# One more batch without PE transposes, and duplicated keys beside kept zeros in a thresholded attention and RWKV feed-forward

## The chip, the cores and the metric

The kernel runs on one core of a Trainium2 chip. A core has five engines that run their own instruction streams side by side: PE (TensorE, matmuls and their weight loads, PEld), DVE (VectorE), ACT (ScalarE), POOL (GpSimd) and SP (SyncE, which here only issues DMA transfers). They meet through semaphores. The metric is the device time of one execution in microseconds; the kernel before takes 974.39 us, the median of three runs (973.27 to 975.24).

## The reference

Two stages follow each other. Eight batches of eight heads, 576 positions, head width 64; then a feed-forward layer of width 512 to 1024 and back over the same 8 x 576 rows.

```python
scores = scale * np.matmul(q, k.transpose(0, 1, 3, 2))
thresh = np.max(scores, axis=-1, keepdims=True) - tau
scores = np.where(scores >= thresh, scores, -1000000000.0)
attn = np.exp(scores - np.max(scores, axis=-1, keepdims=True))
attn = attn / (np.sum(attn, axis=-1, keepdims=True) + 1e-09)
x = np.matmul(attn, v)                      # heads side by side: 512 columns
x_prev = x shifted by one row, zeros first
xk = mu_k * x + (1.0 - mu_k) * x_prev       # xr likewise with mu_r
k = np.maximum(xk @ w_k, 0.0)
out = sigmoid(xr @ w_r) * ((k * k) @ w_v)
```

A score that misses the threshold by a little is dropped altogether, so the scores have to be nearly as exact as float32.

## The kernel before, in words

**Jobs and units.** A job is one batch and one pair of heads (`hp`, four pairs in a batch). Its queries are worked in units: a P unit is 128 query rows for each of the two heads (two softmaxes of 128 x 576), the T unit is the 64 last rows of both heads together (one softmax). A whole job has one T and four P units, so nine softmaxes; a batch has 36 and the program 288. The first `HALF` batches are halved: each of their jobs is cut into two jobs with two P units in the first and T with two P units in the second, which lets the feed-forward of the first 256 rows start early. Before, `HALF` is 2, so there are 16 half jobs and 24 whole ones, 40 in all.

**Scores.** In the first `PLAIN` jobs the scores are plain float32 matmuls straight from the loaded tile `raw` (L600). In the others ACT rounds the tile to the PE's fast type (`hl`, the high part, L510), POOL takes the rest (the low part, L520), and DMA copies stack both parts so that one matmul with 128 rows of contraction does two products. Before, `st1` holds high and low of queries and keys in alternating partitions and `st2` holds the queries with the two parts exchanged; the products are `st1` by `st1` and `st2` by `st1` (L617). T units take another form (L590).

**Softmax of a unit**, per head: row maximum on DVE (L657), threshold on ACT (L665), exponential on ACT (L673), mask, product and sum in one DVE instruction (L681), reciprocal on DVE (L701), scaling on POOL (L710).

**Turning the probabilities.** The matmul with V wants them transposed. Batches below `MOVED` do it on PE: four 128 x 128 transposes for each head of a P unit (L739) into a PSUM tile `w`, which ACT or DVE then copies out into `pm` (L755, L757). Batches from `MOVED` on are "turned" without PE: DVE transposes 32 x 32 blocks of both heads in one instruction (L775; L839 for T), one DMA writes the block rows to DRAM (`far`, `near`; L810, L849), and another reads them back in the order of a full transpose (L815, L860). The tile `pt` that DVE turns into has one buffer (`TB`). A last piece of 64 columns is turned on PE in every unit. Before, `MOVED` is 2, so 24 jobs are turned.

**Attention output and feed-forward.** `attend` multiplies by V (L906). Its result is copied to `xT` by DVE (L757). When the four pairs of a half batch are done, `ffn_chunk` works 256 rows: POOL and ACT mix the rows (L999 to L1045), PE multiplies by `w_k` (L1067, 96 matmuls), `w_r` (L1109, 24) and `w_v` (L1131, 48), with ACT, POOL and DVE between them. A batch has two such chunks, and every four batches one more for the last rows.

**Weights.** 20 pieces of the three weight matrices are fetched and split into high and low parts on POOL, ACT and DVE (L421 to L465) while the first two batches run.

**What sets the order.** Every instruction is first entered as a `Step` with an engine, an expected duration and a key. `Plan.order` then walks through time: on each engine, of the steps whose inputs are there, the one that can start first goes next, and of equals the one with the smaller key. What comes out is a fixed instruction stream for each engine; nothing is reordered on the chip. PE prefers scores, turns and attention (key less 1000) to feed-forward matmuls, so the feed-forward of a batch fills PE while the attention of the next one goes on. Steps at L1191 ("turnstile") transpose the identity for nothing, in the first 100 us of the plan, where PE would otherwise stand idle.

## Time and profile before

| | |
|---|---|
| median of three runs | 974.39 us (973.27 to 975.24) |
| the profiled execution, its own time | 972.76 us |
| span of the trace (first to last instruction) | 970.9 us |
| busy, share of the span | PE 96%, PEld 79%, DVE 71%, ACT 75%, POOL 70% |
| mean granted PE clock | 0.994 of full speed |
| DMA | 227.41 MB, mean 234 GB/s |

The 1.86 us between the span and the execution's own time lie outside the instructions. The chain of work that ended last runs 62% of the span over PE, 17% over DMA, 8% over ACT, 6% over DVE and 3% over POOL. Busy times of a group of instructions are unions of intervals: matmuls overlap, so the time that one more matmul costs is read from the distance of starts, not from the mean length of one.

### The profile page before, as it was taken

To read this page: it belongs to the slowest core of one execution; us is meant where nothing else is said; L and a number is where in the kernel's file an instruction comes from. 1 tells how busy PE (TensorE), PEld (TensorE's weight loads), DVE (VectorE), ACT (ScalarE), POOL (GpSimd) and SP (SyncE) were. 2 spreads that over 40 slices of the span, in tenths; PEclk is the share of its full clock that TensorE was granted. 3 is DMA by queue.
4 is the path that set the end of the run, shared out by engine and by line. 5 is a ranking of instruction groups with operands and counts; after the bars stand their busy time and mean duration, and the time that the engine had idled before them with its cause. 6 is when DMAs were issued, how large, how long until landed. Compare 5 with 4: busy or idle time off the path is not lost.

```text
span 970.9 us, 17935 instructions
## 1 busy us (share of the span) xinstructions
PE 936.5 (96%) x6142; PEld 768.9 (79%) x6142; DVE 689.1 (71%) x1424; ACT 728.7 (75%) x1569; POOL 678.9 (70%) x834
## 2 busy tenths in 40 slices
PE   9888899999999999999999999999999999999998
PEld 8666687887868787878887878788878878878886
DVE  6978897777778687878798868787877777830120
ACT  5899989898777878677868696868777778764432
POOL 3899978676776776958767677676767677664541
PEclk9999999999999999999999999999999999999999
DMA  5696455436768788788878778888778787750000
GB/s 190 235 323 251 150 178 176 161 133 235 267 238 325 275 313 302 279 295 283 299 257 294 240 281 306 278 299 298 276 295 282 262 275 266 266 197 23 22 22 22
DMA packets 91514, 227.41 MB, mean 234 GB/s; under 512 B 8480, under 2 KB 24352, under 8 KB 85280
## 3 DMA queue, kind: packets, MB, share of 16 engines
q1 hardware_dynamic: 91424, 226.27, 66.2%
q8 instruction: 49, 0.80, 0.4%
q14 instruction: 41, 0.34, 0.1%
HBM read 102.77 MB, written 66.06 MB: 174 GB/s over the span
## 4 chain that ended last, share of the span: by engine, by line
PE 62%; DMA 17%; ACT 8%; DVE 6%; POOL 3%; issue 2%; SPq 1%; ACTq 0%; POOLq 0%; DVEq 0%
PE w L1131 14%; PE w L1067 14%; PE w L906 12%; PE s L617 9%; PE w L1109 7%; DMA pm<-far 7%; DMA far<-pt 6%; PE w L739 4%; DVE pt L775 2%; DMA st<-hl 2%; ACT p L673 2%; DMA near<-pt 2%; PE s L590 2%; DVE p L681 1%; PE w L1191 1%
## 5 line engine op out<-in xcount | busy, mean ns | idle before, releaser
L681 DVE SCALAR_TENSOR_TENSOR p<-s,sm,p 128x576 f32<-128x576 f32 x288 | 232.2, 811 | 70.1 <-ACT p L673 68.9
L657 DVE TENSOR_REDUCE sm<-s 128x1 f32<-128x576 f32 x288 | 212.4, 749 | 53.3 <-PE s L617 36.0
L710 POOL TENSOR_SCALAR p<-p,sm 128x576 f32<-128x576 f32 x288 | 212.5, 749 | 38.4 <-DVE sm L701 32.4
L1067 PE MATMUL w<-xk,wk 128*128 128x256 f32 x1728 | 227.9, 283 | 1.7 <-ACT pl L755 1.1
L1067 PEld LDWEIGHTS w<-xk,wk 128*128 128x128 f32 x1728 | 216.4, 188 | 3.7 <-ACT pl L755 1.4
L1131 PE MATMUL w<-wv,k 128*128 128x512 f32 x864 | 219.0, 398 | 0.0
L673 ACT ACTIVATE p<-s,sm 128x576 f32<-128x576 f32 x288 | 210.3, 733 | 8.3 <-DVE pt L775 7.4
L1131 PEld LDWEIGHTS w<-wv,k 128*128 128x128 f32 x864 | 156.8, 189 | 33.3 <-issue 1.8
L906 PE MATMUL w<-pm,v 128*64 128x256 f32 (+1 forms) x1024 | 140.0, 415 | 8.2 <-DMA pm<-far 5.1
L1090 POOL TENSOR_TENSOR k<-r,k 128x512 fp32r<-128x512 f32 x72 | 92.7, 1288 | 51.6 <-ACT k L1080 50.4
L775 DVE STREAM_TRANSPOSE pt<-p 128x1024 f32<-128x1024 f32 x96 | 115.5, 1228 | 17.9 <-DMA near<-pt 8.5
L665 ACT ACTIVATE sm<-sm,small 128x1 f32<-128x1 f32 x288 | 83.3, 290 | 51.5 <-DVE sm L657 50.5
L617 PE MATMUL s<-st 128*128 128x288 f32 x496 | 114.9, 313 | 6.3 <-DVE p L681 5.2
L906 PEld LDWEIGHTS w<-pm,v 128*64 128x64 f32 x1024 | 70.7, 138 | 60.8 <-issue 6.7
L693 POOL TENSOR_SCALAR sm<-sm 128x2 f32<-128x2 f32 (+1 forms) x160 | 30.7, 192 | 115.9 <-DVE p L681 101.8
L1109 PE MATMUL w<-wr,xk 128*128 128x512 f32 x432 | 110.5, 396 | 0.0
L520 POOL TENSOR_TENSOR hl<-raw,hl 128x576 fp32r<-128x576 f32 (+2 forms) x76 | 103.6, 1385 | 9.8 <-ACT hl L510 9.4
L617 PE MATMUL s<-st,st 128*128 128x288 f32 x496 | 109.2, 302 | 0.7 <-DMA st<-hl 0.6
L617 PEld LDWEIGHTS s<-st 128*128 128x128 f32 x496 | 81.3, 190 | 31.8 <-DVE p L681 11.2
L739 PE MATMUL w<-ident,p 128*128 128x128 f32 x448 | 83.9, 284 | 10.2 <-ACT pm L755 3.2
L1109 PEld LDWEIGHTS w<-wr,xk 128*128 128x128 f32 x432 | 76.9, 188 | 14.1 <-issue 0.8
L617 PEld LDWEIGHTS s<-st,st 128*128 128x128 f32 x496 | 79.5, 189 | 2.8 <-issue 1.5
(74 smaller groups left out, 1204.2 us busy)
## 6 DMA issues: line engine op xcount, KB each, us to landing
far<-pt SPq DMA_DIRECT2D x48, 1024.0 KB, 5.6
pm<-far SPq DMA_DIRECT2D x48, 1024.0 KB, 5.7
st<-hl SPq DMA_DIRECT2D x48, 576.0 KB, 4.3
raw<-in_qk SPq DMA_DIRECT2D x24, 608.0 KB, 6.4
v<-in_v SPq DMA_DIRECT2D x40, 320.0 KB, 3.9
st<-hl SPq DMA_DIRECT2D x28, 448.0 KB, 3.2
st<-hl SPq DMA_DIRECT2D x96, 128.0 KB, 3.1
out<-sg SPq DMA_DIRECT2D x32, 256.0 KB, 3.0
```

Of the source, the lines that this page charges most:

```text
L520: lambda cs=cs: G.tensor_tensor(hl.get()[:, 1, cs], raw.get()[:, cs], hl.get()[:, 0, cs].bitcast(F32), op=ALU.subtract),
L617: PE.matmul(ss[y].get()[:, z, 0:HS], l.get()[:, c * P : (c + 1) * P], r.get()[:, keys(y, z)], start=(j == 0), stop=(j == 1),)
L657: lambda sv=sv, col=col: V.tensor_reduce(col(0), sv(), axis=AX.XY, op=ALU.max, negate=True),
L673: lambda sv=sv, pv=pv, col=col: A.activation(pv(), sv(), AF.Exp, bias=col(0)),
L681: lambda sv=sv, pv=pv, col=col: V.scalar_tensor_tensor(pv(), sv(), col(1), pv(), op0=ALU.is_ge, op1=ALU.mult, accum_out=col(2)),
L710: lambda y=y, o=y * S if unit["kind"] == "P" else 0: G.tensor_scalar(p.get()[:, o : o + S], p.get()[:, o : o + S], sm.get()[:, 3, y : y + ...
L739: PE.transpose(pt.get()[:, c, :], x(), ident.get())
L775: V.transpose(o, x)
L906: PE.matmul(o.get()[hs, 0:n], vt.get()[:, c, hs], pt, start=(c == 0), stop=(c == 4))
L1067: PE.matmul(h.get()[:, f], l, r, start=(ct == 0 and i == 0), stop=(ct == NCT - 1 and i == 2))
L1109: PE.matmul(z.get(), l, r, start=(ct == 0 and i == 0), stop=(ct == NCT - 1 and i == 2))
L1131: PE.matmul(vps.get(), l, r, start=(ft == 0 and i == 0), stop=(ft == NFT - 1 and i == 2))
```

## The change

Three parts. First, constants: `HALF` 2 to 1 (batch 1 is no longer halved: 8 half jobs and 28 whole ones), `PLAIN` 2 to 4 (the whole first half of batch 0 has plain scores; its jobs 2 and 3 borrow the buffers of `xk`), `MOVED` 2 to 1 (batch 1 is turned too). Second, the stacked tiles: `st1` now holds high and low of the queries and, behind them, the high part of the keys twice; `st2` holds the low part of the keys in every other partition and zeros between, which are written once by two memsets and kept. The products are `st1` by the doubled keys and `st1` by `st2`, so three of the four products of before are computed and low by low falls away. Third, keys and expected durations of the plan, which give a new order on every engine.

```diff
-MOVED = 2
-PLAIN = 2
+MOVED = 1
+PLAIN = 4
...
-    HALF = 2
-    W0, W1, W2, W3, AVK = 5, 3, 50, 2, 1.5
-    PREP, PB, VB, COLD, EARLY = 12, 3, 1, -1, 30
+    HALF = 1
+    W0, W1, W2, W3, AVK = 3, 4, 60, 1.5, 4.5
+    PREP, PB, VB, COLD, EARLY = 8, 3, 1, -1, 30
...
-        job["st"] = [(sbuf("st1", [P, WM - ST], FR, 3), sbuf("st2", [P, SM], FR, 2)) for _ in range(2)]
+        job["st"] = [(sbuf("st1", [P, SM + S], FR, 3), sbuf("st2", [P, S], FR, 2)) for _ in range(2)]
...
-                    t1.get()[:, 0 : W - qt].bitcast(F32), hl.get()[h::2, :, qt:W].bitcast(F32)
+                    t1.get()[:, 0 : nq - qt].bitcast(F32), hl.get()[h::2, :, qt:nq].bitcast(F32)
...
+            def high(t1=t1, h=h, k0=k0):
+                x = hl.get()[h::2, 0, k0 : k0 + S].bitcast(F32)
+                x = bass.AP(x.tensor, x.offset, [list(x.ap[0]), [0, 2], list(x.ap[1])])
+                SY.dma_start(t1.get()[:, nq - qt : nq - qt + S].bitcast(F32), x)
...
+                    t2.get()[0::2, :].bitcast(F32), hl.get()[h::2, 1, k0 : k0 + S].bitcast(F32)
...
+                        r = st2.get() if j else st1.get()[:, nq - qt : nq - qt + S]
                         PE.matmul(
                             ss[y].get()[:, z, 0:HS],
                             l.get()[:, c * P : (c + 1) * P],
-                            r.get()[:, keys(y, z)],
+                            r[:, z * HS : (z + 1) * HS],
...
                 evict(
-                    *EV[y if n > EARLY else 0],
+                    *EV[y],
...
-    wat = [6 + 1 * j for j in range(len(wlist))]
+    wat = [2 + 3 * j for j in range(len(wlist))]
```

`EV` gives the engine that copies PE transposes out: ACT for head 0, DVE for head 1. Before, ACT took both heads in the first units (`n` up to `EARLY`). `wat` holds the keys of the weight pieces.

**Place 1: PE in the second half of batch 1's scores.** `s` are score tiles, `p` probability tiles, `w` PSUM tiles; L739 before is L761 now (a transpose), L617 is L639, L1131 is L1153, L590 is L611. Before, between softmax 48 and 51:

```order
L739 MATMUL w_97<-ident,p_1654 128x128 x4
L739 MATMUL w_93<-ident,p_1654 128x128 x4
L739 MATMUL w_89<-ident,p_1654 128x128
L617 MATMUL s_128<-st_0_1713 128x288 x2
L617 MATMUL s_128<-st_0_1713,st_0_1695 128x288 x2
L617 MATMUL s_130<-st_1_1735 128x288 x2
L617 MATMUL s_130<-st_1_1735,st_1_1723 128x288 x2
L1109 MATMUL w_97<-wr_0_962,xk_667 128x512 x3
L739 MATMUL w_103<-ident,p_1721 128x128 x4
L739 MATMUL w_89<-ident,p_1721 128x128 x4
L739 MATMUL w_93<-ident,p_1721 128x128
```

Now, between softmax 52 and 54, in the same batch:

```order
L761 MATMUL w_93<-ident,p_1568 128x128
L1153 MATMUL w_101<-wv_0_1687,k_0_1212 128x512 x3
L1153 MATMUL w_101<-wv_0_1692,k_0_1212 128x512 x3
L761 MATMUL w_97<-ident,p_1619 128x128
L761 MATMUL w_93<-ident,p_1668 128x128
L1153 MATMUL w_107<-wv_0_1687,k_0_1212 128x512 x3
L1153 MATMUL w_101<-wv_0_1705,k_0_1212 128x512 x3
L639 MATMUL s_134<-st_1_1289 128x288 x2
L639 MATMUL s_134<-st_0_83,st_1_1289 128x288 x2
L639 MATMUL s_136<-st_2_1484 128x288 x2
L639 MATMUL s_136<-st_1_85,st_2_1484 128x288 x2
```

The groups of four transposes are gone, the single ones for the last 64 columns stay, and `w_v` matmuls of batch 0's feed-forward stand where they were. Counted up to the scores of softmax 73 (the first of batch 2): L739 has 319 transposes before and 182 now; L1067 186 and 192 matmuls, L1109 24 and 48, L1131 48 and 78.

**Place 2: DVE in batch 1.** L657 now L679 is the maximum, L681 now L703 the mask, L757 now L779 a copy out of PSUM, L775 now L797 the turn; L436, L444 and L454 (now L441, L449, L459) belong to a weight piece. Before:

```order
L657 TENSOR_REDUCE sm_1569<-s_130 128x1
L444 SCALAR_TENSOR_TENSOR w_89<-xT_80,w_89 128x512
L681 SCALAR_TENSOR_TENSOR p_1588,sm_1569<-s_128,sm_1569,p_1588 128x576
L454 SCALAR_TENSOR_TENSOR xT_80<-xT_80,w_89 128x512
L757 COPY xT_80<-w_97 128x256
L681 SCALAR_TENSOR_TENSOR p_1588,sm_1569<-s_130,sm_1569,p_1588 128x576
L757 COPY pm_406<-w_89 128x4x4x32
L701 RECIPROCAL sm_1569<-sm_1569 128x2
```

Now:

```order
L679 TENSOR_REDUCE sm_1478<-s_136 128x1
L459 SCALAR_TENSOR_TENSOR xT_80<-xT_80,w_97 128x512
L797 STREAM_TRANSPOSE pt_1422<-p_1368 128x2x4x128
L703 SCALAR_TENSOR_TENSOR p_1429,sm_1398<-s_134,sm_1398,p_1429 128x576
L703 SCALAR_TENSOR_TENSOR p_1499,sm_1478<-s_136,sm_1478,p_1499 128x576
L441 TENSOR_SCALAR w_107<-wv_0_975 128x512
L723 RECIPROCAL sm_1398<-sm_1398 128x2
L679 TENSOR_REDUCE sm_1478<-s_134 128x1
L679 TENSOR_REDUCE sm_1554<-s_136 128x1
```

A turn stands between the masks in place of a copy to `pm`. Up to the mask of softmax 36 DVE has 8 copies out of PSUM and 14 finished weight pieces before, 22 copies (16 of them to `pm`) and 13 pieces now; from there to the mask of softmax 72 it has 31 copies and 6 pieces before, and 15 copies, 7 pieces, 14 turns at L775 and 4 at L839 now.

**Place 3: SP, the stacked tiles and the trips to DRAM.** Before, in the first turned job (batch 2):

```order
L546 DMA st_0_2697<-hl_2632 128x1x1152
L481 DMA raw_2701<-in_qk 128x1216
L849 DMA near_2708<-pt_2703 128x512
L498 DMA v_2715<-in_v 128x640
L860 DMA pm_208<-near_2708 128x4x128
L535 DMA st_0_2774<-hl_2632 64x512 x2
L546 DMA st_1_2784<-hl_2632 128x1x1152
L810 DMA far_2806<-pt_2758 128x2048
```

Now, in batch 1, where its first job is turned and its second and third get their tiles:

```order
L567 DMA st_0_83<-hl_1279 64x576
L549 DMA st_2_1484<-hl_1279 128x1x512
L561 DMA st_2_1484<-hl_1279 128x1x576
L832 DMA far_1518<-pt_1422 128x2048
L567 DMA st_1_85<-hl_1279 64x576
L837 DMA pm_215<-far_1518 128x4x512
L561 DMA st_0_1610<-hl_1598 128x1x576
L549 DMA st_0_1610<-hl_1598 128x1x512
L832 DMA far_1649<-pt_1596 128x2048
L496 DMA raw_1656<-in_qk 128x1216
```

One transfer of 1152 columns and two of half the partitions became one of 512, one of 576 and one of half the partitions for each head. Over the whole program DVE has 16 more turns of L775 and 4 more of L839, SP 16 more of each of L810 and L815 and 4 more of each of L849 and L860; L739 has 144 transposes fewer (448 to 304), copies of them out of PSUM fall from 54 to 20 on ACT and from 18 to 16 on DVE, and the turnstile has 156 transposes in place of 174.

## Rows read from the trace of the kernel before

**Rows 1.** The page's first part: busy time, share of the span and instructions of each engine.

```profile
PE 936.5 (96%) x6142; PEld 768.9 (79%) x6142; DVE 689.1 (71%) x1424; ACT 728.7 (75%) x1569; POOL 678.9 (70%) x834
```

**Rows 2.** Busy time by stretches of the span. Columns: stretch, its length, then for PE, PEld, DVE, ACT and POOL the busy us and the instructions, the granted PE clock, the DMA engines' share and GB/s.

```profile
0.00:54.00 54.00, 47.74 (x340) 37.90 (x340) 40.26 (x87) 39.95 (x89) 35.04 (x51) 1.00 0.63 221
54.00:108.50 54.50, 46.29 (x309) 34.70 (x307) 45.60 (x101) 51.36 (x120) 51.62 (x67) 0.97 0.70 256
108.50:210.70 102.20, 98.81 (x716) 82.13 (x715) 80.99 (x178) 89.45 (x202) 78.67 (x99) 0.98 0.50 169
210.70:316.60 105.90, 102.06 (x653) 82.34 (x652) 81.49 (x164) 83.29 (x181) 75.92 (x94) 0.98 0.71 252
316.60:857.10 540.50, 532.41 (x3495) 438.39 (x3494) 424.06 (x856) 416.33 (x901) 388.43 (x479) 1.00 0.80 281
857.10:970.90 113.80, 109.21 (x641) 93.47 (x639) 16.72 (x46) 48.34 (x81) 49.22 (x48) 1.00 0.15 49
```

**Rows 3.** The same stretches, the masks at L681 alone (each counts twice, with the read of its sum behind it): DVE busy, clock, DMA.

```profile
0.00:54.00 54.00, 13.02 (x32) 1.00 0.63 221
54.00:108.50 54.50, 16.33 (x42) 0.97 0.70 256
108.50:210.70 102.20, 29.40 (x74) 0.98 0.50 169
```

**Rows 4.** The same stretches, the turnstile (L1191) alone: PE and PEld busy, clock, DMA.

```profile
0.00:54.00 54.00, 21.05 (x147) 19.03 (x147) 1.00 0.63 221
54.00:108.50 54.50, 3.56 (x29) 3.10 (x27) 0.97 0.70 256
```

**Rows 5.** PE in order of time around 660 us. Columns: start, length, engine, line, operation, tiles, shape, count.

```profile
658.67 2.38 PE L1067 MATMUL w<-xk,wk 128*128 128x256 f32 x18
660.88 0.43 PE L617 MATMUL s<-st 128*128 128x288 f32 x2
```

**Rows 6.** The same view around 215 us.

```profile
214.56 0.60 PE L739 MATMUL w<-ident,p 128*128 128x128 f32 x4
214.91 0.52 PE L617 MATMUL s<-st 128*128 128x288 f32 x2
215.27 0.43 PE L617 MATMUL s<-st,st 128*128 128x288 f32 x2
215.53 0.43 PE L617 MATMUL s<-st 128*128 128x288 f32 x2
...
216.78 2.31 PE L1109 MATMUL w<-wr,xk 128*128 128x512 f32 x9
219.03 2.37 PE L906 MATMUL w<-pm,v 128*64 128x320 f32 x16
```

**Rows 7.** The same view at a plain job's scores.

```profile
7.71 1.24 PE L600 MATMUL s<-raw 64*128 64x288 f32 x8
8.88 3.82 PE L1191 MATMUL w<-ident 128*128 128x128 f32 x33
```

**Rows 8.** Groups of instructions by line and shape: busy us, mean ns of one, then the idle time before them and what ended it.

```profile
L739 PE MATMUL w<-ident,p 128*128 128x128 f32 x448 | 83.9, 284 | 10.2 <-ACT pm L755 3.2 <-POOL p L710 3.0 <-DVE xT L454 1.6
...
L775 DVE STREAM_TRANSPOSE pt<-p 128x1024 f32<-128x1024 f32 x96 | 115.5, 1228 | 17.9 <-DMA near<-pt 8.5 <-DMA far<-pt 5.3 <-POOL p L710 3.8
...
L755 ACT ACTIVATE pm<-w 128x512 f32<-128x512 f32 x54 | 31.7, 597 | 9.9 <-PE w L739 9.2
...
L839 DVE STREAM_TRANSPOSE pt<-p 128x512 f32<-128x512 f32 x24 | 17.0, 707 | 8.3 <-DMA far<-pt 6.6 <-POOL sm L693 1.0 <-POOL p L710 0.7
...
L454 DVE SCALAR_TENSOR_TENSOR xT<-xT,w 128x512 uint32<-128x512 uint32 x20 | 13.6, 679 | 0.1
...
L757 DVE COPY pm<-w 128x512 f32<-128x512 f32 x18 | 12.4, 687 | 3.2 <-PE w L739 3.0
```

**Rows 9.** Busy time by stretches again, columns as in rows 2, for three stretches of 25 us in the first 150.

```profile
25.00:50.00 25.00, 21.41 (x156) 14.92 (x156) 22.19 (x47) 21.97 (x51) 21.29 (x30) 1.00 0.68 239
...
75.00:100.00 25.00, 19.64 (x118) 15.02 (x117) 22.13 (x49) 23.59 (x55) 23.29 (x31) 0.93 0.59 210
...
125.00:150.00 25.00, 24.63 (x193) 21.58 (x192) 23.41 (x51) 22.41 (x51) 20.00 (x25) 1.00 0.49 166
```

**Rows 10.** Who waited for whom: total us, times, longest us. SPq is the DMA queue of SP.

```profile
DVE pt L775 <- DMA near<-pt: 8.5, 11, 1.4
...
DVE pt L839 <- DMA far<-pt: 6.6, 9, 1.4
...
DVE pt L775 <- DMA far<-pt: 5.3, 8, 1.2
...
PE w L906 <- DMA pm<-far: 5.1, 9, 1.0
...
PE s L617 <- DMA st<-hl: 1.4, 4, 0.6
...
SPq L815 <- DMA far<-pt: 119.6, 39, 6.2
```

**Rows 11.** DMA issues: tiles, queue, count, size of one, median us from issue to landing.

```profile
far<-pt SPq DMA_DIRECT2D x48, 1024.0 KB, 5.6
pm<-far SPq DMA_DIRECT2D x48, 1024.0 KB, 5.7
st<-hl SPq DMA_DIRECT2D x48, 576.0 KB, 4.3
```

More of the change, by code (lines that the diff above doesn't have):

```diff
@@ L81 @@
     HOP, LATE, FROM = 0.09, 0.3, 200.0
-    SOFT = {"DVE": 0.3, "ACT": 0.15, "POOL": 0.2}
-    IDLE = 0.5
+    SOFT = {"DVE": 0.15, "ACT": 0.15, "POOL": 0.2}
+    IDLE = 0.7
     def __init__(self):
@@ L105, in add @@
         s.ready = wait
+        if key > -500 and until is None:
+            s.key += AMP * ((s.idx * 2654435761 + SEED * 40503) % 65536 / 65536 - 0.5)
         def split(x):
@@ L470, in weight @@
         plan.soft = False
+    for j in range(2):
+        t2 = sbuf("st2", [P, S], FR, 2)
+        add("DVE", 0.3, lambda t2=t2: V.memset(t2.get().bitcast(F32), 0.0), writes=[t2], key=-97)
     def operands(job, key):
@@ L476, in operands @@
         W = nq + 2 * ST + SM
-        raw = job["raw"] = sbuf("raw", [P, WM], F32) if job["ji"] != 1 else sbuf("k2", [P, 2 * NFT * CH], F32)
+        raw = job["raw"] = (
+            sbuf("k2", [P, 2 * NFT * CH], F32)
+            if job["ji"] == 1
+            else sbuf("xk", [P, 2 * NCT * CH], F32, 2)
+            if job["ji"] in (2, 3)
+            else sbuf("raw", [P, WM], F32)
+        )
         add(
@@ L612, in scores, with mm @@
             st1, st2 = job["st"][y]
-            for j, l in enumerate((st1, st2)):
-                def mm(j=j, l=l, r=st1, y=y):
+            for j in range(2):
+                def mm(j=j, l=st1, y=y, st1=st1, st2=st2):
                     for z in range(2):
+                        r = st2.get() if j else st1.get()[:, nq - qt : nq - qt + S]
                         PE.matmul(
```

50 lines of the change are left out of this document (25 added, 25 removed).

## The prediction

> **What bounds the kernel now.** I read the page's busy shares first. PE stands at 96% of the span, the next engine at 75% [rows 1]; that alone says little, since lengths of matmuls overlap. So second the busy time by stretches, cut at the batches: the masks count 37 up to 108.5 us and 37 more up to 210.7 us [rows 3], so these are batch 0 and batch 1. From 316.6 to 857.1 us PE is busy 532.4 of 540.5 us [rows 2]. Third the starts on PE: 18 matmuls of the kind L1067 take from 658.67 to 660.88 us, 0.123 us each without a gap [rows 5]. From the third batch on PE is full, and a microsecond of PE work more or less there is a microsecond of time.
>
> The first two batches differ. Up to 108.5 us PE is busy 94.0 us, of which 24.6 us are turnstile, transposes for nothing [rows 2, 4]; it does useful work for about 69 us. There the other engines set the pace: between 75 and 100 us ACT is busy 23.59 of 25 us, POOL 23.29, DVE 22.13 [rows 9]. Over batch 0 ACT has 91.3 us, POOL 86.7, DVE 85.9 [rows 2]: ACT is the fullest, with 17.2 us idle. In batch 1 PE is at 98.81 of 102.2 us, ACT at 89.45, DVE at 80.99.
>
> The Trainium skill (Perfetto Trace Analysis, Identifying the Most-Contended Engine) says that matmul busy time doesn't tell how near PE is to its limit, and takes the busy time of weight loads instead. By that measure PE is at 438.4 of 540.5 us, 81%, from 316.6 us on [rows 2], and removed transposes would fall into free time. The gapless starts of rows 5 speak against it, so it is a rival below, not my reading.
>
> **PE work.** In batch 1, 36 groups of four transposes go (144 of 448). In rows 6 such a group starts at 214.56 and the next instruction at 214.91, 0.35 us; the pair of score matmuls behind it takes 0.36 us to its successor where the next pair takes 0.26. So a group costs 0.35 + 0.10 = 0.45 us, and 36 cost 16.2 us. The bounds are 0.35 (12.6 us) and the busy time over the count, 83.9 us / 448 x 4 = 0.75 (27 us) [rows 8], which counts overlap; I take 0.45. The four units that become plain take 8.88 - 7.71 = 1.17 us [rows 7] where four pairs took 4 x 0.265 = 1.06 [rows 6], together 0.4 us more. The new stacked products have as many matmuls of the same size: nothing. PE gets 15.8 us less to do. Were the time in which it stands or turns idly unchanged, the span would be 970.9 - 15.8 = 955.1 us.
>
> **Whether PE loses more time in the first two batches.** That depends on DVE, which gets the turns. Row durations overlap a little: the page's 689 us of DVE are 0.92 of their sum, so I scale by that.
>
> Batch 0: 16 copies to pm come over from ACT to DVE (0.687 us each, +11.0), two copies to xT (about 0.4) and one weight piece (three instructions like L454, 0.68 each) come later: +8.1, scaled +7.4 us [rows 8]. DVE has 93.3 us, ACT loses those copies (16 x 0.597 = 9.6) and falls to about 82 or below. DVE takes ACT's place with 2 us more work. With ACT's 17.2 us of idleness the batch ends at 110.5 us in place of 108.5.
>
> Batch 1: DVE gets 14 x 1.228 + 4 x 0.707 = 20.0 us of turns before the mask of softmax 72, 2.1 for a weight piece, and loses 16 copies, 11.0: +11.1, scaled +10.2 [rows 8]. That is 81.0 + 10.2 = 91.2 us. DVE has run at 89% and 94% of a stretch when work was at hand (22.19 and 23.41 of 25 us [rows 9]); at 92% the batch takes 99.1 us and ends at 209.6 us, 1.1 before the old 210.7.
>
> PE's work up to the scores of softmax 73 falls by 34 groups (319 to 182 transposes), 15.4 us, and one product with V (16 matmuls of it take 2.37 us [rows 6], and four more belong to it: an estimate of 2.8); it rises by 0.4 and by the feed-forward pulled forward: 6 x 0.12 + 54 x 0.25 (nine L1109 take from 216.78 to 219.03 [rows 6]) = 14.2. Net 3.6 us less work, in 1.1 us less time: PE loses 2.5 us more than before. So batch 1 hardly gets shorter; PE's freed time is spent on batch 0's feed-forward, and the gain appears later, when PE is full and has less left.
>
> Sum: 970.9 - 15.8 + 2.5 = 957.6 us of span. Around it lie 1.86 us in the profiled execution (972.76), whose time is 1.6 under the median 974.39. So 957.6 + 3.5 = 961.1 us.
>
> **Costs taken as nothing, and their cover.** The turnstile's 18 transposes fewer: they filled waiting time. Two memsets of st2: in the first microseconds, when DVE waits for loads; at most about 1 us. ACT and POOL lose work (34 copies of 0.597, and the splitting of halves): neither bounds any more, worth nothing beyond batch 0.
>
> DMA: batch 1 moves 16 x 1 MB and 8 x 0.25 MB more for the turns. The stacked copies fall from 1664 to 1376 KB for a whole job, and halves load their keys twice no longer. That is some 11 MB net in 100 us, 110 GB/s on top of 169 [rows 2]; the later batches run at 252 to 281 GB/s. The trip back is a plain strided copy: 1 MB lands in 5.7 us, the straight one away in 5.6 [rows 11]. The Trainium skill (VectorE: DVE Perf Modes, The three transpose paths) warns that a plain DMA that transposes by strides is 19 times slower when the inner stride of its target is large; here each run is 512 words, and rows 11 show no such cost. By that rule the 5.7 us would be over 100 and no turned job could pay.
>
> Each trip back makes SP wait for the trip away, up to 6.2 us [rows 10], and behind it in SP's order stand the next job's stacked copies and loads. For six batches of this PE waited 1.4 us for stacked tiles and 5.1 us for pm [rows 10], so one batch more costs about 1 us. DVE waits for pt's one buffer 8.5 + 5.3 + 6.6 = 20.4 us in six batches, 3.4 in one; that lies in the 8% idleness of batch 1. The new stacked tiles let the first product start before the low part of the keys is there; worth between 0 and 1.4 us, taken as 0.
>
> The clock: it shows 0.93 between 75 and 100 us [rows 9], worth 25 x 0.07 = 1.75 us of full speed at most, and 0.97 to 0.98 in three stretches of rows 2. With less turnstile one such spell more or less is possible: 2 us to either side.
>
> **Rivals.** *Early start (20%).* DVE is denser than ACT was: 12 us idle in batch 0 and 95% in batch 1 give 105.3 + 96.0 = 201.3 us, and PE's lost time falls by 5.8 instead of rising by 2.5: 953 us. For it: four plain jobs spare the copies and splits that the first jobs waited for. Against it: DVE waited for ACT's exponentials in batch 0 as well.
>
> *DVE as the bound (8%).* In batch 1 a mask waits for the exponential and a turn for pt to be emptied, and DVE doesn't get denser than it is now there, 81.0 of 102.2 us, 79%. Then 91.2 us take 115.1, batch 1 ends at 225.6, PE loses 18.5 us more and the time is 977.1. The point from which it decides: 15.8 us of lost time, batch 1 ending 12.2 us after 210.7, that is DVE under 81% of it. For it: 78% in the later batches as well [rows 2]. Against it: there PE was the bound and DVE had time to spare.
>
> *The transposes ran in free time (12%).* The weight-load measure, or a half of the gain given back in waits for trips and a drained feed-forward: batch 1's feed-forward is ready only after all four whole jobs now. Full loss is 974, half of it 968.
>
> **Numbers.** The forecast has 60%, with 956 to 969 as its own range: DVE at 94% in batch 1 with 15 us idle before gives 957, at 85% 969. This kernel's runs lie within 0.2% (about 2 us), so that is what can be told from no change. Faster by more: 60 + 20 + half of the 12, 86%. Within: 6%. Slower: 8%. The range for 8 in 10 goes from 951 to 973 us.
>
> **What would show it.** Right: L739 with 304 transposes and PE's stretch after 316 us as full as before; DVE the fullest engine of batch 0 and batch 1, near 92% of the latter; batch 1 ending within some 5 us of 210 us with about 60 more feed-forward matmuls done; a span near 958. Wrong: PE with gaps of many microseconds between 110 and 220 us that end on pm's trip back or on DVE's masks; a stretch behind 316 us in which PE is less dense than 98%; or batch 0 ending before 102 us.

## The result and the profile after

The changed kernel takes 983.06 us (median of five runs, 979.38 to 983.82) where the kernel before takes 973.27 us beside it (971.57 to 975.24). The ratio is 1.0085, with an interval of 1.0064 to 1.0106: it is slower by about 10 us, and the forecast was 961.1 us with a range of 951 to 973. The profiled execution took 983.06 us with a span of 981.3. One run of all those in this document, fit2's profiled one at 980.31 us, counts as a slow one: it is left out of fit2's time, and the work and lost times read from it carry no argument.

The page's first part for the changed kernel answers to [rows 1]:

```profile
PE 933.2 (95%) x5980; PEld 753.1 (77%) x5980; DVE 707.7 (72%) x1444; ACT 707.2 (72%) x1525; POOL 669.3 (68%) x822
```

The groups by line and shape, of the changed kernel (columns as in [rows 8]):

```profile
L761 PE MATMUL w<-ident,p 128*128 128x128 f32 x304 | 67.7, 294 | 12.0 <-POOL p L732 5.4 <-ACT pm L777 1.3 <-DVE pm L779 1.3
```

The 144 transposes are gone, and yet PE's busy time fell by 3.3 us only (936.5 to 933.2). A busy time can't tell work from slow work, so I counted PE another way for every kernel below. I call **work** the sum over PE's matmuls, each priced at the distance to its successor where matmuls follow each other without a gap at the full clock (0.117 us for 128 x 256, 0.230 for 512 columns, 0.132 for a score matmul, 0.109 for a transpose, 0.142 or 0.1155 for a product with V of 320 or 256 columns, 0.146 for a plain score, 0.085 more where a transpose or product with V gives way to another kind, nothing for the turnstile). **Lost** is the span up to the last matmul's start less that work: waiting, turnstile, and slow clock together. Before, work is 879.4 us and lost 86.5; after, 862.6 and 113.3. So PE has 16.8 us less to do, about as forecast, and loses 26.8 more. The level of these figures hangs on the prices: taken strictly as listed they give 895.4 and 878.2 us of work, and as much less lost. The differences between kernels, which all that follows uses, stay the same within some 1 us in every stretch. By stretches of the span:

| us lost in | 0-108 | 108-324 | 324-540 | 540-870 | from 870 |
|---|---|---|---|---|---|
| before | 47.7 | 16.6 | 7.8 | 13.4 | 0.9 |
| after | 51.0 | 28.4 | 21.0 | 11.4 | 1.5 |
| difference | +3.3 | +11.8 | +13.2 | -2.0 | +0.6 |

The first three columns hold it all. The windows of the changed kernel (columns as in [rows 2]; the first rows are taken at the old times, then come batch 1 up to its true end, the spell of slow clock, and two stretches of the table):

```profile
0.00:54.00 54.00, 49.25 (x328) 36.36 (x329) 44.76 (x97) 36.69 (x81) 33.85 (x49) 1.00 0.50 177
54.00:108.50 54.50, 46.37 (x289) 33.61 (x289) 47.88 (x104) 48.26 (x115) 47.91 (x62) 0.88 0.73 265
...
316.60:857.10 540.50, 525.50 (x3407) 427.73 (x3404) 423.41 (x852) 409.42 (x889) 382.90 (x473) 0.99 0.77 268
857.10:981.30 124.20, 118.84 (x718) 101.60 (x716) 23.18 (x58) 53.53 (x93) 53.82 (x54) 0.99 0.18 63
108.50:217.40 108.90, 100.42 (x642) 80.18 (x641) 91.16 (x182) 83.69 (x182) 77.94 (x97) 0.98 0.68 235
100.00:110.00 10.00, 8.47 (x36) 4.66 (x34) 6.30 (x14) 8.28 (x17) 8.88 (x12) 0.53 0.42 148
...
108.00:324.00 216.00, 201.11 (x1289) 160.17 (x1286) 174.60 (x349) 163.62 (x360) 153.67 (x192) 0.97 0.74 258
324.00:540.00 216.00, 204.08 (x1320) 164.74 (x1319) 166.13 (x332) 159.73 (x346) 150.14 (x186) 0.98 0.75 264
```

The same two stretches of the kernel before:

```profile
108.00:324.00 216.00, 208.76 (x1412) 171.11 (x1409) 168.16 (x348) 179.64 (x398) 161.61 (x200) 0.98 0.61 211
324.00:540.00 216.00, 213.40 (x1382) 174.69 (x1381) 172.05 (x359) 167.46 (x359) 154.77 (x193) 1.00 0.81 288
```

From 324 to 540 us both kernels work on whole, turned jobs; PE's matmuls are of the same kinds and sizes in both, and only the stacked tiles under the scores differ. There PE starts 1320 instructions in place of 1382 and every other engine has fewer too: all engines get less done, without any of them being fuller.

The masks at L703 show where the batches end (each counts twice, as in [rows 3]: 72 are a batch):

```profile
54.00:108.50 54.50, 16.27 (x40) 0.88 0.73 265
...
108.50:217.40 108.90, 28.66 (x72) 0.98 0.68 235
```

Up to 108.5 us 32 and 40 masks are done, 36 softmaxes; the last of them ends at about 107 us. The next 36 end at 217.4 us, so batch 1 takes 110.4 us where 99.1 were forecast and 102.2 were needed before.

What PE waits for, over the whole span of the changed kernel (total us, times, longest):

```profile
PE s L639 <- DVE p L703: 14.1, 15, 2.3
PE w L928 <- DMA pm<-far: 10.3, 9, 3.1
```

The same two waits in the stretch where each is largest: the first from 108 to 324 us, after and before, then the second from 324 to 540 us, after and before:

```profile
PE s L639 <- DVE p L703: 9.5, 8, 2.3
PE s L617 <- DVE p L681: 2.2, 3, 1.7
...
PE w L928 <- DMA pm<-far: 7.2, 3, 3.1
PE w L906 <- DMA pm<-far: 1.5, 3, 0.6
```

The longest wait for a trip back, in PE's order of time, with the wait in brackets:

```profile
338.74 0.43 PE L639 MATMUL s<-st,st 128*128 128x288 f32 x2
342.24 3.29 PE L928 MATMUL w<-pm,v 128*64 128x256 f32 x16 [3.07 <-DMA pm<-far]
```

And SP's queue ahead of it:

```profile
326.59 0.32 SPq L832 DMA_DIRECT2D far<-pt  x1
329.02 0.34 SPq L1169 DMA_DIRECT2D out<-sg  x1
329.80 0.53 SPq L561 DMA_DIRECT2D st<-hl  x1
331.30 0.53 SPq L549 DMA_DIRECT2D st<-hl  x1
332.81 0.34 SPq L496 DMA_DIRECT2D raw<-in_qk  x1
333.20 1.50 SPq L837 DMA_DIRECT2D pm<-far  x1
```

The trip back of 1 MB goes out 0.4 us behind a load of 608 KB and is there 9.0 us later (333.20 to 342.24). That is the slowest of them: of the 56 trips, the 22 that go out next after a load take 7.2 us in the median and the 26 next after a stacked copy 5.7. But this was so in the kernel before (18 behind a load, 7.6 us; 12 behind a stacked copy, 5.7). The median of all trips back, 6.1 us, is only 0.4 us above that of [rows 11]:

```profile
far<-pt SPq DMA_DIRECT2D x56, 1024.0 KB, 5.2
pm<-far SPq DMA_DIRECT2D x56, 1024.0 KB, 6.1
```

All of PE's waits listed between 108 and 540 us come to 26.2 us after and 9.4 before, so 16.8 of the 25.0 us more that it lost there. The clock has most of the rest: 0.97 and 0.98 in the two stretches against 0.98 and 1.00, which on 216 us each is some 6 us of full speed. Over the span the mean granted clock is 0.984 against 0.994, 10 us of full speed at most. In the ten microseconds from 100 us it was 0.53, so nearly all the time at the lower of its two levels, 1.2 of 2.4 GHz. PE's order of time ahead of that:

```profile
97.66 0.53 PE L639 MATMUL s<-st 128*128 128x288 f32 x2 [1.50 <-DVE p L703]
...
99.31 1.09 PE L761 MATMUL w<-ident,p 128*128 128x128 f32 x4
101.18 1.30 PE L761 MATMUL w<-ident,p 128*128 128x128 f32 x5 [0.78 <-ACT pm L777]
103.21 1.09 PE L761 MATMUL w<-ident,p 128*128 128x128 f32 x4 [0.73 <-DVE pm L779]
```

PE stood 1.50 us for a mask, and soon four transposes take 1.09 us where [rows 6] have 0.60; further waits of 0.8 and 0.7 us follow while the clock is low. At the end of the 3.07 us wait above the clock is at the lower level too (columns as in [rows 2]):

```profile
341.50:345.00 3.50, 2.76 (x14) 1.60 (x16) 2.13 (x2) 0.63 (x1) 2.63 (x3) 0.51 0.28 89
```

### The profile page after: what moved, and what is told of

Read it like the earlier page. It is cut to its first block, busy times and chain, and to the rows that moved or that the text cites. A ratio compares the mean times of both kernels' runs of the same rounds, so it can differ in the third digit from the quotient of the medians.

```text
span 981.3 us, 17443 instructions
## 1 busy us (share of the span) xinstructions
PE 933.2 (95%) x5980; PEld 753.1 (77%) x5980; DVE 707.7 (72%) x1444; ACT 707.2 (72%) x1525; POOL 669.3 (68%) x822
## 4 chain that ended last, share of the span: by engine, by line
PE 61%; DMA 12%; DVE 9%; ACT 8%; POOL 6%; issue 3%; SPq 0%; POOLq 0%; ACTq 0%; DVEq 0%
PE w L1089 17%; PE w L1153 12%; PE w L928 11%; PE s L639 9%; PE w L1131 8%; DMA pm<-far 6%; DMA far<-pt 3%; DVE p L703 3%; ACT p L695 2%; DVE pt L797 2%; PE w L761 2%; POOL hl L535 2%; PE s L611 2%; DVE sm L679 2%; DMA near<-pt 2%
## 5 line engine op out<-in xcount | busy, mean ns | idle before, releaser
L703 DVE SCALAR_TENSOR_TENSOR p<-s,sm,p 128x576 f32<-128x576 f32 x288 | 231.1, 809 | 57.6 <-ACT p L695 56.7
L679 DVE TENSOR_REDUCE sm<-s 128x1 f32<-128x576 f32 x288 | 211.5, 748 | 49.0 <-PE s L639 32.9
L1153 PE MATMUL w<-wv,k 128*128 128x512 f32 x864 | 216.9, 398 | 0.8 <-POOL wv L470 0.8
L1153 PEld LDWEIGHTS w<-wv,k 128*128 128x128 f32 x864 | 157.5, 189 | 34.1 <-POOL wv L470 1.3
L928 PE MATMUL w<-pm,v 128*64 128x256 f32 (+1 forms) x1024 | 147.4, 430 | 13.4 <-DMA pm<-far 10.3
L797 DVE STREAM_TRANSPOSE pt<-p 128x1024 f32<-128x1024 f32 x112 | 135.0, 1228 | 20.5 <-DMA near<-pt 13.5
L639 PE MATMUL s<-st 128*128 128x288 f32 x480 | 111.9, 315 | 14.7 <-DVE p L703 14.1
L639 PEld LDWEIGHTS s<-st 128*128 128x128 f32 x480 | 77.8, 190 | 44.4 <-DVE p L703 28.8
L1131 PE MATMUL w<-wr,xk 128*128 128x512 f32 x432 | 111.7, 397 | 0.0
L639 PE MATMUL s<-st,st 128*128 128x288 f32 x480 | 106.0, 302 | 0.0
L535 POOL TENSOR_TENSOR hl<-raw,hl 128x576 fp32r<-128x576 f32 (+1 forms) x64 | 92.7, 1462 | 17.7 <-ACT hl L525 13.6
L1131 PEld LDWEIGHTS w<-wr,xk 128*128 128x128 f32 x432 | 77.3, 189 | 14.2 <-issue 0.5
L777 ACT ACTIVATE pl<-w 128x128 f32<-128x128 f32 (+1 forms) x192 | 48.9, 255 | 49.2 <-PE w L761 47.3
L1097 ACT ACTIVATE r<-w 128x512 f32<-128x512 f32 x72 | 43.0, 597 | 54.1 <-POOL k L1112 29.6
```

The costliest lines, as they stand in the source:

```text
L535: lambda cs=cs: G.tensor_tensor(hl.get()[:, 1, cs], raw.get()[:, cs], hl.get()[:, 0, cs].bitcast(F32), op=ALU.subtract),
L639: PE.matmul(ss[y].get()[:, z, 0:HS], l.get()[:, c * P : (c + 1) * P], r[:, z * HS : (z + 1) * HS], start=(j == 0), stop=(j == 1),)
L679: lambda sv=sv, col=col: V.tensor_reduce(col(0), sv(), axis=AX.XY, op=ALU.max, negate=True),
L703: lambda sv=sv, pv=pv, col=col: V.scalar_tensor_tensor(pv(), sv(), col(1), pv(), op0=ALU.is_ge, op1=ALU.mult, accum_out=col(2)),
L797: V.transpose(o, x)
L928: PE.matmul(o.get()[hs, 0:n], vt.get()[:, c, hs], pt, start=(c == 0), stop=(c == 4))
```

## The experiments

My theory after the result: the new order loses the time, not the tiles or the turns as such. Rivals: turning batch 1 makes DVE the bound there and costs what it saves; the new stacked tiles cost more than the old; the trips back suffer from the queue of SP. They have these results (medians; ratio to the kernel before, run beside each on the same chip; work and lost as above, of the profiled execution, which for nb_down was 11 us faster than the median):

```
kernel          us       ratio [95%]             work   lost   0-108 108-324 324-540 540-870  870+
e1_stack         996.86  1.0234 [1.0178,1.0290]  879.8  110.9   44.8   21.8    16.8    26.2    1.3
e2_struct       1006.28  1.0334 [1.0268,1.0400]  863.1  134.0   44.4   35.2    27.2    25.8    1.3
e3_plan          985.90  1.0124 [1.0065,1.0183]  879.8  100.1   44.6   16.7    16.8    20.6    1.3
e4_stack_struct  996.80  1.0258 [1.0177,1.0339]  863.8  122.8   45.2   40.8    19.8    15.6    1.4
b_j1            1074.69  1.1069 [1.1030,1.1109]  880.2  187.5   45.1   38.4    28.4    55.1   20.5
b_j2            1063.57  1.0952 [1.0912,1.0992]  879.9  175.9   50.3   21.3    29.4    45.1   29.8
a_j1            1067.81  1.0994 [1.0950,1.1038]  862.8  195.6   46.5   43.3    30.6    48.2   27.0
a_j2            1079.39  1.1103 [1.1059,1.1147]  863.4  210.0   45.2   48.7    37.6    47.4   31.2
r_raw           1024.79  1.0531 [1.0480,1.0582]  862.6  149.2   47.8   41.1    25.7    32.1    2.5
fit1             960.95  0.9868 [0.9834,0.9902]  862.9   90.4   44.6   25.9     8.9    10.4    0.6
fit2             976.59  1.0012 [0.9977,1.0048]  863.5  109.9   40.8   35.4    15.8    16.5    1.4
fit3             973.71  1.0027 [1.0004,1.0050]  863.3  101.3   52.6   21.9    13.7    12.4    0.8
e5_unturned      966.32  0.9919 [0.9889,0.9948]  879.4   77.6   50.3    9.3     6.8    10.5    0.6
fit_unturned     961.83  0.9893 [0.9862,0.9923]  879.6   78.2   41.8    9.9    14.1    11.2    1.2
nb_up            993.33  1.0214 [1.0130,1.0299]  879.5  106.8   51.2   12.9    20.1    21.1    1.4
nb_down         1011.27  1.0357 [1.0276,1.0439]  879.3  114.2   49.1   17.9    20.8    23.9    2.4
na_up            992.13  1.0167 [1.0093,1.0241]  863.1  124.0   51.3   28.9    25.2    17.2    1.5
na_down          992.00  1.0177 [1.0104,1.0250]  862.5  119.6   43.1   41.9    22.9    10.2    1.5
```

### The parts apart

**e1_stack**: the kernel before with the new stacked tiles alone (the tiles `st1`, `st2`, their copies and products as in the change's diff).

```diff
-        job["st"] = [(sbuf("st1", [P, WM - ST], FR, 3), sbuf("st2", [P, SM], FR, 2)) for _ in range(2)]
+        job["st"] = [(sbuf("st1", [P, SM + S], FR, 3), sbuf("st2", [P, S], FR, 2)) for _ in range(2)]
```

> The kernel before with the new stacked tiles alone (queries, doubled high keys, low keys beside kept zeros); constants and keys of the plan as before. Order theory (the new keys of the plan are what costs): no change, 973 us within 4. Copy theory (the new stacked copies crowd the DMA queue and make the trips back late): 978 us or more, and PE waits over 8 us for pm where it waited 5.1.

**e2_struct**: the kernel before with the three numbers of structure alone (jobs 2 and 3 get their `raw` from the buffers of `xk`).

```diff
-MOVED = 2
-PLAIN = 2
+MOVED = 1
+PLAIN = 4
...
-    HALF = 2
+    HALF = 1
```

> The kernel before with the three counts alone: one halved batch, four plain jobs, batch 1 turned; stacked tiles and keys as before. Order theory: the forecast gain shows, 958 to 966 us. Turning theory (batch 1 is then bound by DVE and the feed-forward of batch 1 comes too late): 973 us or more, with PE's lost time between 108 and 324 us up by 10 us or more.

**e3_plan**: the kernel before with the new keys and constants of the plan alone. With them goes the line on `EV`: 14 copies to `pm` move from ACT to DVE. Some of the changed keys aren't shown below.

```diff
-    SOFT = {"DVE": 0.3, "ACT": 0.15, "POOL": 0.2}
-    IDLE = 0.5
+    SOFT = {"DVE": 0.15, "ACT": 0.15, "POOL": 0.2}
+    IDLE = 0.7
...
-                 pipe = max(pipe, t) + s.kb / 350.0
+                 pipe = max(pipe, t) + s.kb / 335.0
...
-    W0, W1, W2, W3, AVK = 5, 3, 50, 2, 1.5
-    PREP, PB, VB, COLD, EARLY = 12, 3, 1, -1, 30
+    W0, W1, W2, W3, AVK = 3, 4, 60, 1.5, 4.5
+    PREP, PB, VB, COLD, EARLY = 8, 3, 1, -1, 30
...
-    KADD, KTHR = 0, 0
-    KMAX, KEXP, KMASK = -1, 0, 2
+    KADD, KTHR = 0.5, 0
+    KMAX, KEXP, KMASK = 1, 1, 2
...
-                    *EV[y if n > EARLY else 0],
+                    *EV[y],
...
-    wat = [6 + 1 * j for j in range(len(wlist))]
+    wat = [2 + 3 * j for j in range(len(wlist))]
...
```

> The kernel before with the plan's new keys and durations alone. Order theory: 983 us or more, with long waits for pm between 300 and 540 us. Turning theory and copy theory: 973 us within 4.

**e4_stack_struct**: the first two together, with the old keys and constants.

> The kernel before with stacked tiles and counts, but its old keys; the changed kernel less its new keys. Order theory: 957 to 966 us. Turning and copy theories: 978 us or more, like the changed kernel's 983.

Measured: each part by itself is slower than the kernel before, by 2.3, 3.3 and 1.2%, and the parts are not additive; all three together cost 0.9%. The order theory has only e3_plan right; e1_stack, e2_struct and e4_stack_struct came out on the side of its rivals, with 17.2 us of waits for `pm` in e1_stack and 35.2 us lost from 108 to 324 us in e2_struct. PE's waits, first in e1_stack (its attention is at L917), then in e2_struct, then in e3_plan, from a row of the waits each:

```profile
PE w L917 <- DMA pm<-far: 17.2, 14, 3.6
```

```profile
PE s L617 <- DVE p L681: 13.8, 13, 2.8
PE w L906 <- DMA pm<-far: 11.7, 11, 3.2
```

```profile
PE w L906 <- DMA pm<-far: 13.3, 8, 3.4
```

[rows 10] had 5.1 us for the trips back. e3_plan executes the instructions of the kernel before in another order, but for the 14 copies and 18 more idle transposes, all in the first 112 us. PE's work is the same within 0.4 us. It loses 3.1 us less up to 108 us and 16.2 us more behind 324, where the instructions are the same, so that loss is the order's. In e1_stack and e2_struct the order moves too, since new steps enter the same plan: neither for the order theory nor against it can they price the tiles or the turns. Whether the stacked tiles by themselves cost anything these runs don't tell.

### Is the order of before an exceptional one?

**b_j1, b_j2** (kernel before) and **a_j1, a_j2** (changed kernel): every key moved by up to 0.1 either way, two patterns each.

```diff
+        if key > -500 and until is None:
+            s.key += AMP * ((s.idx * 2654435761 + SEED * 40503) % 65536 / 65536 - 0.5)
```

> The kernel before, the same work, with every key of the plan moved by a pseudo-random amount of up to 0.1 to either side (seed 1; scores, turns and attention on PE keep theirs), so only the order among near equals changes. Lucky-order theory (the order of before is an unusually good one, and any change leaves it): 985 to 1000 us, PE's work the same 879 us, its lost time 100 us or more. Rival (the changed counts and tiles cost by themselves): 973 us within 4.

> The same with seed 2. Lucky-order theory: 985 to 1000 us. Rival: 973 us within 4.

> The changed kernel with its keys moved by up to 0.1 (seed 1). Lucky-order theory: the mean over the seeds lies 10 to 17 us under that of the moved orders of before, each between 972 and 992 us. Rival: 983 us within 4, and above the moved orders of before.

> The same with seed 2. Lucky-order theory: between 972 and 992 us. Rival: 983 us within 4.

Measured: 9 to 11% slower, far outside what either theory said. The windows from 860 us to the end, of b_j1 and then of the kernel before (columns as in [rows 2]):

```profile
860.00:1073.00 213.00, 196.60 (x1166) 166.69 (x1162) 45.63 (x101) 93.70 (x172) 96.61 (x97) 0.97 0.19 67
```

```profile
860.00:971.00 111.00, 106.31 (x617) 90.61 (x615) 15.40 (x44) 46.33 (x78) 46.77 (x45) 1.00 0.14 48
```

1166 PE instructions are left at 860 us in place of 617. In the code many feed-forward steps share one key and go by the order in which they were entered; the jitter mixes them. That the feed-forward is late for this reason is my reading, but the rows suffice to say that these runs are no measure of neighbouring orders. The runs tell only that the changed kernel under the same jitter loses 43.3 and 48.7 us from 108 to 324 us where the other loses 38.4 and 21.3.

**nb_up, nb_down, na_up, na_down** ask the same with a smaller step: the rate in KB/us that the plan assumes for a DMA, 350 in the kernel before and 335 in the changed one. The chip's transfers are what they were; only the order moves.

```diff
-                pipe = max(pipe, t) + s.kb / 350.0
+                pipe = max(pipe, t) + s.kb / 355.0
```

(345.0 in nb_down; 340.0 and 330.0 for 335.0 in na_up and na_down.)

> The kernel before, its plan assuming a DMA rate of 355 KB per us in place of 350; same instructions, a neighbouring order. Lucky-order theory: slower than before by 8 us or more (981 to 1000), PE's lost time over 95 us against 86.5. Counts theory (the changed counts and tiles lose the time whatever the order): 973 us within 4.

> The kernel before with an assumed rate of 345. Lucky-order theory: 981 to 1000 us. Counts theory: 973 us within 4.

> The changed kernel, its plan assuming 340 in place of 335. Lucky-order theory: as good or bad as the changed kernel, 970 to 995 us, and the mean of both neighbours not above that of the neighbours of before. Counts theory: 983 us within 4.

> The changed kernel with an assumed rate of 330. Lucky-order theory: 970 to 995 us. Counts theory: 983 us within 4.

Measured: a step of 1.4% in an assumed rate costs the kernel before 2.1% up and 3.6% down, the changed kernel about 0.9% either way (1.0167 and 1.0177 against 1.0085). So the order of before stands some 20 to 38 us below its neighbours and that of the changed kernel 9. The neighbours differ from their kernels by as much as the change does, or more: 993 and 1011 us with the old instructions, 992 twice with the new. All four came out on the side of the lucky-order theory (nb_down above its range), none within the counts theory's 4 us; but these are two neighbours of each kernel. PE's waits of nb_down, then those of na_up, then na_up's clock:

```profile
PE s L617 <- DVE p L681: 13.9, 16, 1.9
PE w L906 <- DMA pm<-far: 6.3, 6, 2.2
```

```profile
PE s L639 <- DVE p L703: 21.0, 20, 4.2
```

```profile
core 0: 992.1 us, clock 0.973
```

### The queue of SP

**r_raw**: the changed kernel, where a load of `raw` that stands one or two transfers ahead of a trip back is issued behind it; 23 of 28 loads move.

```diff
...
+                dma = [k for k in range(j + 1, len(out)) if self.steps[out[k]].eng == "DMA"][:2]
+                back = [k for k in dma if self.steps[out[k]].kind == "back"]
+                if back:
+                    users = [k for k in range(j + 1, back[0] + 1) if out[j] in self.steps[out[k]].deps]
+                    if not users:
+                        out.insert(back[0], out.pop(j))
...
```

> The changed kernel in its own order, but each load of the next job's queries and keys (608 KB) that stands on SP within two transfers ahead of a trip back to pm is issued right behind that trip: 23 of 28 loads move, nothing else. Queue theory (the trips back are late because they queue behind such loads): PE's waits for pm fall from 10.3 + 10.8 us to about 8 together and the time by 5 us or more, to 978 or below. Whole-order theory (the waits are spread over the order): 983 us within 4.

Measured: 1024.79 us, where neither theory had it. Three rows of the waits:

```profile
ACT raw L521 <- DMA raw<-in_qk: 63.8, 25, 5.4
...
PE s L656 <- DVE p L720: 30.6, 25, 3.7
...
PE w L946 <- DMA pm<-far: 2.7, 4, 1.2
```

PE's wait for trips falls from 10.3 to 2.7 us, as the queue theory had it. That the queue caused those waits isn't shown by it: the median trip back lands in 6.0 us where it took 6.1, and PE itself comes later to it, since its waits for masks rise from 14.1 to 30.6 us. What is shown is that the loads had no slack. A load moved behind a trip back waits for the trip away as well, since SP does (42 times, 103.5 us in all), and ACT now stands 25 times for 63.8 us where it waited once, 3.2 us. In this queue the time given to one transfer was taken from another.

### The same instructions in another order

**fit1**: the changed kernel with eight constants of the plan set anew (the expectation says seven; the diff shows eight). No instruction is added, removed or resized other than turnstile transposes, which the plan sets where it sees PE idle. The plan sets 42 more of these in fit1 (198 for 156). fit1, fit2, fit3 and fit_unturned are sets that the plan itself prefers by its own durations; how many sets they were taken from isn't on record.

```diff
-    HOP, LATE, FROM = 0.09, 0.3, 200.0
-    SOFT = {"DVE": 0.15, "ACT": 0.15, "POOL": 0.2}
-    IDLE = 0.7
+    HOP, LATE, FROM = 0.09, 0.25, 200.0
+    SOFT = {"DVE": 0.15, "ACT": 0.1, "POOL": 0.2}
+    IDLE = 0.6
...
-    W0, W1, W2, W3, AVK = 3, 4, 60, 1.5, 4.5
+    W0, W1, W2, W3, AVK = 3, 3.5, 60, 1.5, 4.0
...
-    KTURN, KMOVE, RB, DMOVE, TB, FB = 0, 4, 2, 0.35, 1, 4
-    KADD, KTHR = 0.5, 0
+    KTURN, KMOVE, RB, DMOVE, TB, FB = -1, 6, 2, 0.35, 1, 4
+    KADD, KTHR = 0.0, 0
```

> The changed kernel's instructions with seven constants of its plan set anew (keys of turns, trips and sums, three durations, two times of weights and attention). Whole-order theory (the changed counts and tiles save their 16 us of PE work, and the order gave it back): 962 to 976 us, PE's work 863 us as in the changed kernel and its lost time 95 to 105 instead of 113. Rival (batch 1's turning costs by itself, whatever the order): 980 us or more, with 25 us or more of lost time between 108 and 324 us as in the changed kernel.

**fit2** has thirteen constants different (the expectation says eleven), among them the rate at 340 and `AVK` at 5.5.

> The same with another set of constants (eleven of them). Whole-order theory: 962 to 976 us. Rival: 980 us or more.

**fit3** has eight, among them the rate at 345, `W0` at 7 and `W1` at 2.5.

> The changed kernel's instructions with a third set of eight constants. Order theory: 958 to 977 us; lost time between 108 and 324 us 22 to 35 us as in every kernel in which batch 1 is turned, under 25 us between 324 and 860 us.

Measured: fit1 takes 960.95 us, 22 us less than the changed kernel with the same work, and beats both kernels (0.9868 of before, 0.9834 to 0.9902). fit2 comes to 976.59 in runs from 965.54 to 979.90, fit3 to 973.71, 1.0012 and 1.0027 of the kernel before. So the order alone, with its 42 idle transposes, is worth 22 us, over twice the result's size; and a set that the plan likes doesn't always do as well on the chip. The whole-order theory has the side of these times right and not its ranges, since fit1 lies just under 962 us and fit2 just over 976. Of the rival the time is refuted, but its sign, 25 us or more lost from 108 to 324 us, is there in fit1 (25.9; fit3 has 21.9). fit1's page, its windows, PE's waits and its clock:

```profile
PE 925.6 (97%) x6022; PEld 751.8 (78%) x6022; DVE 702.8 (73%) x1444; ACT 707.9 (74%) x1525; POOL 669.3 (70%) x822
```

```profile
108.00:324.00 216.00, 202.63 (x1290) 160.28 (x1289) 178.70 (x357) 168.10 (x369) 157.99 (x195) 0.98 0.76 270
324.00:540.00 216.00, 212.45 (x1398) 173.83 (x1397) 177.65 (x372) 168.15 (x366) 157.26 (x198) 1.00 0.80 281
...
105.00:207.00 102.00, 95.73 (x611) 76.21 (x609) 89.71 (x181) 84.34 (x186) 79.12 (x97) 0.98 0.68 240
```

```profile
PE s L639 <- DVE p L703: 9.0, 13, 2.0
PE w L928 <- DMA pm<-far: 4.7, 6, 1.6
```

```profile
core 0: 958.4 us, clock 0.994
```

From 324 to 540 us PE starts 1398 instructions, more than before (1382), and the clock is back. But from 108 to 324 us it starts 1290, one more than the slow order: fit1 mends the later stretch and the start (44.6 us lost in place of 51.0), and batch 1 only a little (25.9 lost in place of 28.4).

### Does turning batch 1 pay?

**e5_unturned**: the changed kernel with batch 1's transposes back on PE.

```diff
-MOVED = 1
+MOVED = 2
```

> The changed kernel with batch 1 turned by PE transposes again (24 turned jobs, not 28), all else as changed. Turning theory: faster than the changed kernel by 8 us or more though PE has 16 us more to do, because the lost time up to 324 us falls by over 20. Whole-order theory: a new order of either sort, 975 to 1000 us.

**fit_unturned**: the same with a set of constants that the plan prefers for it (`LATE` 0.1, `FROM` 275, `IDLE` 0.5, `W0` 1, `W2` 50, `KADD` 2, `KMASK` 1.5, `wat` from -1 by 4, one key 5 less).

> The changed kernel with batch 1 turned on PE (24 turned jobs) and ten constants of the plan set anew. PE has 16.5 us more to do than in the kernel that did best so far (961 us). If turning pays once the order fits: 968 us or more. If its gain is taken back by DVE in batches 1 and 2 in every order: 950 to 963 us, with PE's lost time between 108 and 324 us under 12 us.

Measured: e5_unturned takes 966.32 us, 17 us less than the changed kernel, though PE's work is 16.8 us more: what the turning theory expected (the time lost up to 324 us falls by 19.8 us where it had over 20), and below the 975 us of the whole-order theory. Its windows:

```profile
108.00:324.00 216.00, 212.69 (x1452) 175.08 (x1450) 170.87 (x355) 178.23 (x390) 159.06 (x198) 1.00 0.53 183
324.00:540.00 216.00, 213.81 (x1398) 174.97 (x1394) 175.88 (x366) 165.50 (x360) 155.35 (x193) 1.00 0.80 277
```

PE is dense from 108 us on, at a granted clock of 1.00, and loses 9.3 us up to 324 us where the changed kernel loses 28.4. This pair differs by the turns alone, and by the order that the plan makes of them. The two sets that fit best differ in other constants too; there it is 25.9 against 9.9. That is 16 to 19 us, about the 16.8 us of PE work that the turns save. fit1 and fit_unturned end at 960.95 and 961.83 us, with intervals that overlap. So in these runs turning batch 1 gains nothing that shows, with one fitting order for each. My theory was half of it: the order loses time, and so does the turning. What makes fit1 and fit_unturned faster than the kernel before, the rest of the change or an order that suits it, isn't shown: the kernel before was not given such a set of constants.

## Why the prediction was wrong, point by point

**PE's work: right.** 15.8 us less were forecast, 16.8 counted. The count prices matmuls by distances of starts as the forecast did, so it bears out the counting and is no second measure of the price of a group.

**Transposes in free time: not refuted by times.** This rival had the kernel at 968 to 974 us. fit1 and fit_unturned, with and without batch 1's transposes on PE, end alike, as it would have it. What speaks against its mechanism is where the freed time goes, to waits: in fit1 PE waits 9.0 us for masks, in fit_unturned 1.9, and over batch 1 PE is busy 99.25 of 101 us in e5_unturned, the row below, and 95.73 of 102 in fit1. One of the two measures that the Trainium skill takes for the matmul engine (Perfetto Trace Analysis, Identifying the Most-Contended Engine), the busy time of weight loads, reads 80.57 us in that row, 80%, so by it a fifth would be free. No run here filled that fifth, so the reading is neither borne out nor refuted.

```profile
105.00:206.00 101.00, 99.25 (x703) 80.57 (x702) 81.68 (x178) 86.61 (x192) 74.16 (x94) 0.98 0.30 103
```

**Batch 0: a little better than forecast.** It was to end at 110.5 us and ended at 107, with DVE at 91.9 us up to there against 93.3. PE nevertheless lost 3.3 us more up to 108 us, since the slow clock (0.88 where [rows 2] have 0.97) fell into it.

**DVE's share in batch 1: wrong.** DVE's work of 91.2 us was right (91.9 from 107.0 to 217.4 us), the 92% were not: it came to 83%, and 88% in fit1 (89.71 of 102 us). I had taken the share from 25-us windows of the first two batches [rows 9], in which DVE made no turns. With the turns PE's lost time rose by 11.8 us from 108 to 324 us, after 3.3 up to 108, and not by 2.5 in all. Two small misreadings don't matter: each batch has 36 softmaxes and not the 37 read from [rows 3], where a mask across the end of a stretch counts on both sides, and DVE's busy time is 0.90 of the sum of its durations and not 0.92, which moves the forecast of batch 1's end by some 0.4 us. This is the rival "DVE as the bound" in part: it decided at 81%. In batch 1 no engine is full, and the waits go round: in the changed kernel from 107 to 217.4 us POOL waits 15.1 us for masks, ACT 11.1 us for DVE's maxima, and DVE 6.6 us for ACT's exponentials. That a turn of 1.2 us between two masks delays the ring is my reading; no run changed that alone.

**"From the third batch on PE is full": the step that failed.** I let a microsecond less of PE work be a microsecond of time after 316 us, as if any order would keep PE as dense as the old one did. From 324 to 540 us the changed kernel loses 21.0 us in place of 7.8, with PE's matmuls there of the same kinds and sizes, and fit1 8.9 with the same instructions. The prediction's own sign of being wrong came true: from 316.6 to 857.1 us PE is busy 525.5 of 540.5 us, 97%, where it was 98.5%. PE is full there only in an order that keeps it so. With the losses up to 324 us as measured and this stretch as before, the span would be 970.9 - 16.8 + 3.3 + 11.8 = 969.2 us, a kernel slightly faster; the 13.2 us make it slower. The prediction's own sum says the same: with batch 1's true end, 6.7 us behind the old one, PE loses 6.7 + 3.6 = 10.3 us more and the time is 955.1 + 10.3 + 3.5 = 968.9 us, inside the range. So DVE's share and this step failed by similar amounts, and it is this one that takes the time out of the range.

**Trips back: too low.** About 1 us was forecast for one batch more; PE waited 10.3 us in place of 5.1, and 7.2 of them from 324 to 540 us, behind the batch that is newly turned. The longest wait, 3.1 us, came where a load went out just ahead; the longest in [rows 10] was 1.0. The number of trips was right in the forecast: 8 more away and 8 more back of 1 MB (48 to 56 of each), not the 16 more of each line that the part on the change counts. The stretch's loss is more than these waits, though. The trip back takes 6.1 us for 1 MB against 5.2 for the trip away. The Trainium skill (VectorE: DVE Perf Modes, The three transpose paths) has a plain copy that transposes by strides 19 times slower than the chip's own transposing DMA when the innermost stride at the target is large. No run here makes such a DMA, so the prediction's "over 100" us, which set the 19 against a straight copy, has nothing here to be held against.

**The clock: too narrow.** 2 us to either side were allowed; the fall from 0.994 to 0.984 is worth up to 10 us. It goes with waits, but loosely: PE's waits come to 41 us in the changed kernel (clock 0.984), 48 in na_up (0.973), 69 in r_raw (0.985) and 43 in nb_up (0.992). fit1 is at 0.994 with 42 idle transposes more; but they end at 81 us, and the changed kernel's longest spell at the lower clock begins at 99 us, with no idle transposes near it in either kernel. From 324 to 540 us neither has any, and the clock is 1.00 in fit1 against 0.98.

**Early start** didn't happen in the changed kernel (batch 1 ends at 217.4, not 201.3); in fit1 it ends at 208 us.

The forecast time of 961.1 us is that of fit1. That the sum fits there doesn't save it: it is luck in part, since fit1 lost 9.3 us more from 108 to 324 us than the kernel before and got two thirds of it back at the start and after 540 us.

What stays open: which of the eight constants makes fit1 fast, whether the kernel before would do as well with constants that fit it, what the new stacked tiles cost alone, and how much of the change's gain without the turns lies in plain jobs, the unhalved batch or the order (e5_unturned and the kernel before have the same work and differ by 7 us).

## What to carry to other kernels

An order made by a planner can be one lucky draw: price a change of structure against the neighbours of the old order as well as against the old order itself, and allow for the spread between them (here 1 to 4%). An engine that is full is full in this order; a saving on it is time only if the new order feeds it as well, so widen the range by that spread and search the order again before judging the change. Work moved from a full engine to one at 80% wasn't free here, where the engines wait for each other's results: take such an engine's share from a stretch that holds the same mix of operations.
